# A residual rebuilt on GpSimd from two kept parts, in place of a DRAM copy, in a fused attention and gated-MLP kernel

## Chip, cores and metric

One core of one Trainium2 chip. The metric is the device time of one execution in microseconds (us). The kernel before took 342.78 us, the median of 3 runs (342.32 to 345.28).

## What is computed

Four batches; each has 12 heads of causal attention (448 positions, head size 64), whose output x (768 features of 448 positions) goes through a gated MLP with a residual. `f` below stands for the tanh form of GELU.

```
attn = softmax(mask(q @ k.T / 8)) @ v            # per batch and head
x    = attn as [448, 768]
h    = f(x @ w_in);  u, v = h[:, :512], h[:, 512:]
vn   = (v - mean(v)) / sqrt(var(v) + 1e-6) * g_ln
vs   = w_sg @ vn + b_sg[:, None]
out  = x + (u * vs) @ w_out
```

## The kernel before

The 48 heads go in 24 pairs (0 to 23, six a batch); a pair gives 128 of the 768 feature rows of x. For a pair: one load of q and k (L428); scores on TensorE (PE, L435) in two halves; masked maxima on VectorE (DVE, L450); exponentials on ScalarE (ACT, L458), ten a pair; the inverse sums go through DRAM (rd, L477) and come back spread over the partitions (rb, L480). The probabilities must then be transposed. Pairs 0 to 7 do it on PE (L502) with copies by ACT and DVE. Pairs 8 to 23 use two block transposes on DVE (L490) into one shared buffer (P_92 in the orders below), and four DMAs from it into a slot of B (L494, two slots). PE multiplies B by the values (L528, the "o" matmuls), and DVE scales the result by rb into a tile xt (L555). So from pair 8 on a pair's transposes wait for the four DMAs of the pair before to land, and its DMAs wait for the o matmuls of the pair two before, which held the slot of B.

`keep_x` then keeps a pair's x in two float32r parts, a high part (a rounded copy, by GpSimd, POOL, at L562 in batch 0 and by ACT at L564 later) and a low part (POOL, L565 for 448 columns, L567 for 64 more), in one of six slots. Both parts feed the MLP's matmuls as split products. Beside that, a DMA writes x to a DRAM tile xd (L560).

The MLP of a batch is made of matmul groups (all L584): v groups (`win,x`, 512 wide), u groups (`x,win`, 448), s groups (`wsg,vn`) and o groups (`g,wout`). For the output of each 128 feature rows (`mc`, six a batch) an o group runs on PE, and DVE adds the residual to it (L704). Two mc share one tile `res`: it is read back from xd by a DMA (L692, 448 KB; two slots, in the last batch the slots of qk), added to, and written out (L712 in pairs of mc, in the last batch L708 one by one, its last mc in two halves of 224 columns). Gating uses POOL at L678 and L681.

Nothing is scheduled while it runs. The operations are recorded with their dependences, and a table of numbers, ORDER, gives the order in which they are issued; each engine works its own part of that order strictly one after the other, and so does the DMA queue of SyncE (SP), which issues every load and store. An issue that waits holds up all issues behind it.

Of the kernel before, what the change touches and what calls it, by code (L numbers as in the profile page):

```python
# [8 lines left out]
F32 = mybir.dt.float32  # L9
# [4 lines left out]
ALU = mybir.AluOpType  # L14
# [214 lines left out]
def attention_gated_mlp(ctx: ExitStack, tc: tile.TileContext, qk, vP, w_in, g_ln, w_sgT, b_sg, w_out, out):  # L229
# [47 lines left out]
    rT = [const.tile([8, 128], F32, name=f"rT{i}") for i in range(NS)]  # L277
    pad = const.tile([128, 8], F32, name="pad")
    rd = [dram.tile([128, 128], F32, name=f"rd{i}") for i in range(NS)]
    xd = dram.tile([B, DM, S], F32, name="xd")  # L280

    od = Order(slots)

# [484 lines left out]
```

## Time and profile before

The profile is of one execution of 343.92 us; its span, first to last instruction, is 342.1 us.

| | before |
|---|---|
| median of 3 runs | 342.78 us |
| profiled execution, its span | 343.92 us, 342.1 us |
| PE busy | 328.2 us (96%) |
| DVE, ACT, POOL busy | 256.8, 198.1, 148.5 us |
| DMA queue of SP | 69.06 MB, 68.6% of the 16 engines' span |

Read it in this order: how much PE idles, where, and what ended the idling; then which work stands right ahead of those places in the chain of waits; then what the touched instructions take.

### The profile page before, as it was taken

What the parts mean: (1) busy time and instruction counts of PE and PEld (TensorE: products, weight loads), DVE (VectorE), ACT (ScalarE), POOL (GpSimd) and SP (SyncE); (2) the same over time, 40 slices, a digit from 0 to 9 for tenths busy, and PEclk for the clock granted to TensorE, in tenths of its full rate; (3) what the DMA queues carried; (4) which work ended last, traced back from release to release, by engine and by line L of the source; (5) the groups of instructions that cost most, each with busy time, mean ns of one, the idle gap of its engine ahead of it and who ended that gap; (6) DMA issues with size and microseconds to landing.
All of it is one profiled execution on the core that took longest, in us unless ns stands there. A gap on an engine that the chain in (4) does not pass through costs nothing.

```text
span 342.1 us, 7655 instructions
## 1 busy us (share of the span) xinstructions
PE 328.2 (96%) x2614; PEld 266.9 (78%) x2615; DVE 256.8 (75%) x762; ACT 198.1 (58%) x658; POOL 148.5 (43%) x201
## 2 busy tenths in 40 slices
PE   3998989999999999999999999999998999999995
PEld 2666567777987887878888978878887987799995
DVE  4899887899999899979879776989577431477513
ACT  2999897896657756566644853753562601243410
POOL 4467586678779700302342901202226623142550
PEclk9999999999999999999999999999999999999999
DMA  7979878787688987788698789747676656005304
GB/s 231 347 241 294 273 243 272 209 306 218 170 224 236 283 236 225 223 229 222 164 290 234 225 225 266 205 119 160 187 199 199 192 129 194 0 2 188 107 2 161
DMA packets 37975, 69.55 MB, mean 203 GB/s; under 512 B 3888, under 2 KB 18992, under 8 KB 37936
## 3 DMA queue, kind: packets, MB, share of 16 engines
q1 hardware_dynamic: 37936, 69.06, 68.6%
q8 instruction: 21, 0.34, 0.4%
q14 instruction: 18, 0.15, 0.1%
HBM read 39.68 MB, written 12.58 MB: 153 GB/s over the span
## 4 chain that ended last, share of the span: by engine, by line
PE 79%; ACT 6%; DMA 6%; DVE 4%; issue 1%; SPq 1%; POOL 1%; DVEq 0%; POOLq 0%; ACTq 0%
PE m L584 58%; PE o L528 10%; PE s L435 9%; ACT P L458 4%; DMA vn<-in_w_in_dram 2%; DMA qk<-in_qk_dram 2%; DMA B<-P 2%; PE ty L502 1%; PE tx L502 1%; ACT B L509 1%; ACT vn L370 1%; PE s L472 1%; DVE P L490 1%; SPq L494 1%; DVE s L450 1%
## 5 line engine op out<-in xcount | busy, mean ns | idle before, releaser
L458 ACT ACTIVATE P<-s,ngm 64x64 f32<-64x64 f32 (+3 forms) x240 | 100.4, 429 | 33.2 <-DVE ngm L450 18.3
L450 DVE CUSTOM_DVE_ANT_0 s<-s,mask 128x192 f32<-128x192 f32 (+3 forms) x192 | 77.3, 438 | 8.3 <-PE s L435 7.2
L584 PE MATMUL m<-win,x 128*128 128x512 f32 (+1 forms) x264 | 65.4, 397 | 0.0
L584 PE MATMUL m<-g,wout 128*128 128x448 f32 x288 | 62.0, 369 | 0.0
L584 PE MATMUL m<-x,win 128*128 128x448 f32 x288 | 61.6, 367 | 0.0
L584 PEld LDWEIGHTS m<-x,win 128*128 128x128 f32 x288 | 53.6, 188 | 4.9
L584 PEld LDWEIGHTS m<-g,wout 128*128 128x128 f32 x288 | 53.3, 188 | 5.2
L584 PEld LDWEIGHTS m<-win,x 128*128 128x128 f32 (+1 forms) x264 | 47.1, 183 | 11.3
L435 PE MATMUL s<-qk 64*64 64x64 f32 (+5 forms) x768 | 47.3, 376 | 6.1 <-DMA qk<-in_qk_dram 5.5
L435 PEld LDWEIGHTS s<-qk 64*64 64x64 f32 x768 | 30.4, 140 | 24.4 <-issue 10.4
L458 ACT ACTIVATION_READ_ACCUMULATOR P<-s,ngm 128x1 f32 (+1 forms) x240 | 48.6, 202 | 0.0
L528 PE MATMUL o<-B,vraw 128*64 128x64 f32 (+4 forms) x672 | 45.9, 291 | 1.3 <-issue 1.0
L528 PEld LDWEIGHTS o<-B,vraw 128*64 128x64 f32 x672 | 33.5, 137 | 15.1 <-issue 6.3
L490 DVE STREAM_TRANSPOSE P<-P 128x1024 f32<-128x1024 f32 x32 | 38.5, 1226 | 5.5 <-DMA vraw<-in_vP_dram 2.9
L584 PE MATMUL m<-wsg,vn 128*128 128x448 f32 x176 | 39.0, 368 | 0.3 <-DVE vn L641 0.3
L628 POOL TENSOR_TENSOR mv<-mv,mhalf 128x1 f32<-128x1 f32 (+1 forms) x16 | 10.4, 648 | 58.7 <-DVE mv L626 52.2
L584 PEld LDWEIGHTS m<-wsg,vn 128*128 128x128 f32 x176 | 32.7, 188 | 3.5 <-issue 0.6
L565 POOL TENSOR_TENSOR x<-xt,x 128x448 fp32r<-128x448 f32 x24 | 27.8, 1166 | 17.3 <-ACT x L564 17.0
L595 ACT ACTIVATE tmp<-tmp 128x448 f32<-128x448 f32 (+2 forms) x32 | 19.2, 603 | 16.2 <-DVE tmp L593 15.9
L678 POOL TENSOR_TENSOR tmp<-tmp,g 128x448 f32<-128x448 f32 x16 | 18.2, 1144 | 23.9 <-DVE tmp L674 16.3
L593 DVE SCALAR_TENSOR_TENSOR tmp<-tmp,m 128x448 f32<-128x448 f32 (+1 forms) x28 | 17.6, 632 | 12.3 <-ACT tmp L592 12.2
L450 DVE DVE_READ_ACCUMULATOR2_ANT ngm<- 128x1 f32 (+1 forms) x192 | 26.2, 136 | 0.0
(77 smaller groups left out, 363.0 us busy)
## 6 DMA issues: line engine op xcount, KB each, us to landing
B<-P SPq DMA_DIRECT2D x64, 256.0 KB
qk<-in_qk_dram SPq DMA_DIRECT2D x24, 448.0 KB
vn<-in_w_in_dram SPq DMA_DIRECT2D x12, 512.0 KB
vraw<-in_vP_dram SPq DMA_DIRECT2D x24, 256.0 KB
rb<-rd SPq DMA_DIRECT2D x24, 256.0 KB
xd<-xt SPq DMA_DIRECT2D x24, 224.0 KB
res<-xd SPq DMA_DIRECT2D x9, 448.0 KB
out_dram<-res SPq DMA_DIRECT2D x9, 448.0 KB
```

Source lines behind the costliest of these rows:

```text
L435: nc.tensor.matmul(out=s[z][bk].t[64 * h:64 * h + 64, col:col + n], lhsT=qk_.t[r, 0, q0:q0 + 64], rhs=qk_.t[r, 1, k0:k0 + n], start=True, ...
L450: nc.vector.tensor_tensor_reduce(out=o, in0=i, in1=mk, scale=-0.125, scalar=3e38, op0=ALU.add, op1=ALU.min, accum_out=ngm[ib[z]][c][0:m])
L458: act(n, lambda c=c, m=m, k0=k0, n=n, bk=bk, col=col, off=off, kc=kc, i=i, z=z: nc.scalar.activation(out=P[i][0:m, off:off + n], in_=s[z][ ...
L490: dve(PW, lambda z=z: nc.vector.transpose(A[ia][:, :, :, z, :].rearrange("p g t k -> p t g k"), P[ib[z]]), Pk[z] + [kp], Ak, 1.105)
L502: nc.tensor.transpose(out, P[ib[z]][:, col:col + 128], ident)
L528: nc.tensor.matmul(out=dst(o.t[r]), lhsT=vr.t[:, c, r], rhs=src(z), start=first and n == 0, stop=last and n == len(lst) - 1)
L565: pool_tt(S, lambda: nc.gpsimd.tensor_tensor(out=y.t[:, S + 64:], in0=x.t, in1=f(y.t)[:, 0:S], op=ALU.subtract), [x, y], [(y, 1)])
L584: nc.tensor.matmul(out=ps.t[0:l().shape[1], 0:n], lhsT=l(), rhs=rr(), start=(k == 0), stop=(k == len(mms) - 1))
L593: dve(n, lambda: nc.vector.scalar_tensor_tensor(out=z(), in0=z(), scalar=1.0 / GC, in1=h(), op0=ALU.add, op1=ALU.mult), [ps], [t])
L595: act(n, lambda: nc.scalar.activation(out=z(), in_=z(), func=AF.Tanh, scale=GS * GC), [], [t], True)
L628: od.add("pool", 0.46, lambda mv=mv, m=m: nc.gpsimd.tensor_tensor(out=mv.t[0:m, 1:2], in0=mv.t[0:m, 1:2], in1=mhalf[0:m], op=ALU.pow), ["s ...
L678: pool_tt(S, lambda z=z, u=u: nc.gpsimd.tensor_tensor(out=z(), in0=z(), in1=u.t, op=ALU.mult), [u], [t])
```

## The change

xd goes. `keep_x` no longer writes x to DRAM (24 DMAs of 224 KB), and the residual is no longer read back (12 DMAs of 448 KB). Instead POOL adds the high and the low part of a pair's x into its half of `res` (L691 of the changed kernel, 24 additions of 128x448), and DVE's L704 waits for that half. `res` has three slots in all batches, the last one included. The rb tile is 448 columns instead of 512. A slot of x is now free once the matmuls and the addition have read it.

```diff
-    xd = dram.tile([B, DM, S], F32, name="xd")
...
-        rb, sb = buf(some[SLOTS["rb"]], "rb", [128, 512]), s[1][1]
+        rb, sb = buf(some[SLOTS["rb"]], "rb", [128, S]), s[1][1]
...
-        dma(lambda: nc.sync.dma_start(out=xd[b, hp * 128:(hp + 1) * 128, :], in_=x.t), [x], [("xd", b, hp)], 229e3)
...
-                rr = buf(*((two, "res") if b < B - 1 else (some[SLOTS["qk"]], "qk")), [128, 2, S])
-                dma(lambda rr=rr, d2=d2: nc.sync.dma_start(out=rr.t, in_=xd[b, d2, :].rearrange("(a p) s -> p a s", a=2)),
-                    [("xd", b, mc), ("xd", b, mc + 1)], [rr], 459e3)
+                rr = buf(three, "res", [128, 2, S])
+                for k in range(2):
+                    x = xhl[b, mc + k]
+                    pool_tt(S, lambda rr=rr, x=x, k=k: nc.gpsimd.tensor_tensor(
+                        out=rr.t[:, k, :], in0=f(x.t)[:, 0:S], in1=f(x.t)[:, S + 64:], op=ALU.add), [x, (x, 1)], [(rr, k)],
+                            ring=[rr])
...
-                    [ps, rr], [(rr, 2 * k + z)])
+                    [ps, (rr, z)], [(rr, 2 + 2 * k + z)])
...
-    4, 1, 2, 84, 85, 0, 89, 87, 90, 88, 86, 93, 91, 12, 13, 96, 95, 98, 97, 94, 100, 102, 14, 92, 101, 99, 15, 16, 17,
+    0, 2, 84, 1, 4, 85, 87, 86, 89, 88, 90, 91, 93, 92, 12, 14, 94, 13, 15, 127, 128, 132, 130, 129, 16, 17, 95, 96,
```

The table ORDER is new from its first to its last number (1927 before, 1915 now), so every engine has another order. Three places matter below.

**SP, the moves of the last two pairs into B.** `B<-P_92` is one of a pair's four DMAs into its slot of B, `x2` and `x4` so many behind one another; vraw is a load of values, rd and rb the inverse sums. Before, the stretch with the moves of pairs 22 and 23:

```order
L560 DMA xd<-xt 128x448
L494 DMA B<-P_92 128x1x512 x2
L560 DMA xd<-xt 128x448
L522 DMA vraw<-in_vP_dram 128x512 x2
L692 DMA res<-xd 128x2x448
L494 DMA B<-P_92 128x1x512 x2
L477 DMA rd_128<-rT_124 4x16x128 x2
L480 DMA rb<-rd_128 128x1x512
L494 DMA B<-P_92 128x1x512 x4
L560 DMA xd<-xt 128x448
```

and now, pairs 20 to 23:

```order
L492 DMA B<-P_92 128x1x512 x4
L426 DMA qk<-in_qk_dram 128x896
L492 DMA B<-P_92 128x1x512 x4
L475 DMA rd_126<-rT_122 4x16x128 x2
L475 DMA rd_128<-rT_124 4x16x128 x2
L478 DMA rb<-rd_128 128x1x448
L478 DMA rb<-rd_126 128x1x448
L492 DMA B<-P_92 128x1x512 x4
L520 DMA vraw<-in_vP_dram 128x512 x2
L712 DMA out_dram<-res 128x2x448
L492 DMA B<-P_92 128x1x512 x4
```

Before, pair 22's four moves stood in two pieces with a write to xd, two value loads and a read of `res` between; now each of the last four pairs has its four moves in one piece. Of the 16 pairs five had their moves in pieces before, three have now.

**PE, where pairs 12, 13 and 14 are multiplied.** `o_2284` before and `o_2258` now are pair 13's o matmuls; `o_2270` is pair 14's (`o_2465` before, which follows only 29 rows below the end of this piece). Before:

```order
L584 MATMUL m_2256<-x_1426,win_87 128x448 x3
L584 MATMUL m_2260<-x_1426,win_87 128x448 x3
L584 MATMUL m_2233<-x_1975,win_87 128x448 x3
L584 MATMUL m_2256<-x_1428,win_87 128x448 x3
L528 MATMUL o_2284<-B_2047,vraw_2034 64x256 x2
L528 MATMUL o_2284<-B_2047,vraw_2034 64x128 x2
L528 MATMUL o_2284<-B_2047,vraw_2034 64x64 x2
L528 MATMUL o_2284<-B_2047,vraw_2034 64x256 x2
L528 MATMUL o_2284<-B_2047,vraw_2034 64x64 x2
L528 MATMUL o_2284<-B_2047,vraw_2034 64x128 x2
L528 MATMUL o_2284<-B_2047,vraw_2034 64x64 x4
L435 MATMUL s_2305<-qk_2092 64x448
```

and now:

```order
L581 MATMUL m_2245<-x_1453,win_87 128x448 x3
L581 MATMUL m_2245<-x_1456,win_87 128x448 x3
L581 MATMUL m_2245<-x_1845,win_87 128x448 x3
L581 MATMUL m_2245<-x_1909,win_87 128x448 x3
L526 MATMUL o_2258<-B_2101,vraw_2015 64x256 x2
L526 MATMUL o_2258<-B_2101,vraw_2015 64x128 x2
L526 MATMUL o_2258<-B_2101,vraw_2015 64x64 x2
L526 MATMUL o_2270<-B_2227,vraw_2268 64x256 x2
L526 MATMUL o_2270<-B_2227,vraw_2268 64x128 x2
L526 MATMUL o_2270<-B_2227,vraw_2268 64x64 x2
L526 MATMUL o_2258<-B_2101,vraw_2015 64x256 x2
L526 MATMUL o_2258<-B_2101,vraw_2015 64x64 x2
```

Pair 14's o matmuls have moved up, in between those of pair 13. Between the last o matmul of pair 12 and the first of pair 14 there stand now one pair's scores, 9 matmuls 512 wide, 24 matmuls 448 wide (eight rows of three), one small `s<-ident,rs` and the first six o instructions of pair 13. Pair 11 too is multiplied earlier after its scores: between them stand now the scores of pairs 12, 13 and half of 14, 48 matmuls 448 wide and pair 10's o matmuls.

**POOL, the end of the last batch.** `tmp` and `g` rows are the gating, `res` rows the new additions. Before, the last eight rows of work:

```order
L678 TENSOR_TENSOR tmp_3880<-tmp_3880,g_3825 128x448
L681 TENSOR_TENSOR g_3909<-tmp_3880,g_3907 128x448
L678 TENSOR_TENSOR tmp_3902<-tmp_3902,g_3876 128x448
L681 TENSOR_TENSOR g_3958<-tmp_3902,g_3956 128x448
L678 TENSOR_TENSOR tmp_3933<-tmp_3933,g_3900 128x448
L681 TENSOR_TENSOR g_3976<-tmp_3933,g_3974 128x448
L678 TENSOR_TENSOR tmp_3937<-tmp_3937,g_3905 128x448
L681 TENSOR_TENSOR g_3981<-tmp_3937,g_3979 128x448
```

and now, the last eleven:

```order
L675 TENSOR_TENSOR tmp_3881<-tmp_3881,g_3821 128x448
L678 TENSOR_TENSOR g_3892<-tmp_3881,g_3890 128x448
L675 TENSOR_TENSOR tmp_3902<-tmp_3902,g_3856 128x448
L675 TENSOR_TENSOR tmp_3922<-tmp_3922,g_3886 128x448
L678 TENSOR_TENSOR g_3925<-tmp_3902,g_3905 128x448
L675 TENSOR_TENSOR tmp_3934<-tmp_3934,g_3888 128x448
L678 TENSOR_TENSOR g_3937<-tmp_3922,g_3927 128x448
L678 TENSOR_TENSOR g_3941<-tmp_3934,g_3939 128x448
L691 TENSOR_TENSOR res_3678<-x_3206 128x448
L691 TENSOR_TENSOR res_3997<-x_3631 128x448
L691 TENSOR_TENSOR res_3997<-x_3636 128x448
```

Three of the 24 additions stand behind all gating. On SP the last seven stores were three of 448 columns, the two halves of 224, and two more of 448; now the five of 448 come first and the two halves last.

## Rows read from the trace of the kernel before

**Rows 1.** The page: engine, busy us (share of span), instructions.

```profile
PE 328.2 (96%) x2614; PEld 266.9 (78%) x2615; DVE 256.8 (75%) x762; ACT 198.1 (58%) x658; POOL 148.5 (43%) x201
```

**Rows 2.** Windows: stretch, length, busy us (instructions) by engine, PEclk, DMA share, GB/s.

```profile
12.00:21.00 9.00, 8.38 (x74) 5.58 (x72) 8.16 (x34) 9.00 (x33) 3.97 (x5) 1.00 0.84 274
21.00:46.00 25.00, 22.23 (x252) 15.33 (x251) 21.98 (x85) 23.88 (x95) 15.97 (x20) 1.00 0.87 277
46.00:100.00 54.00, 54.00 (x402) 42.06 (x401) 49.93 (x154) 42.53 (x135) 40.12 (x55) 1.00 0.76 231
...
250.00:300.00 50.00, 48.70 (x345) 41.25 (x343) 24.04 (x53) 15.87 (x42) 18.04 (x21) 1.00 0.53 147
...
330.00:342.10 12.10, 8.62 (x43) 7.65 (x41) 3.78 (x7) 0.00 (x0) 0.98 (x1) 0.94 0.32 115
```

**Rows 3.** PE's waits: line, waited for, us in total, times, longest.

```profile
PE tx L502 <- ACT P L458: 1.2, 1, 1.2
PE o L528 <- issue: 1.0, 1, 1.0
...
PE o L528 <- DMA B<-P: 0.3, 1, 0.3
```

**Rows 4.** Chain that ended last: start us, us, what.

```profile
34.79 7.49 DMA vn<-in_w_in_dram
...
108.52 2.45 PE s L435 x32
...
200.85 2.44 PE m L584 x12
203.29 3.68 PE o L528 x64
...
214.62 10.46 PE m L584 x45
...
257.53 1.04 issue
...
279.45 5.85 DMA B<-P
...
287.42 51.21 PE m L584 x245
338.66 0.62 DVE qk L704
```

**Rows 5.** Timeline of SP's queue: start us, us, instruction, count.

```profile
122.72 3.20 SPq L494 DMA_DIRECT2D B<-P  x4
...
260.96 1.20 SPq L494 DMA_DIRECT2D B<-P  x2
...
266.25 1.20 SPq L494 DMA_DIRECT2D B<-P  x2
...
276.93 4.11 SPq L494 DMA_DIRECT2D B<-P  x4
...
333.84 5.81 SPq L708 DMA_DIRECT2D out_dram<-qk  x7
```

**Rows 6.** Lines L560, L692: ns min/median/max, first and last start.

```profile
L560 SPq DMA_DIRECT2D xd<-xt x24: 325/613/1614, 32.5 to 311.7; - x24
L692 SPq DMA_DIRECT2D res<-xd x9: 371/434/917, 58.7 to 287.0; - x9
```

**Rows 7.** Groups of POOL: line, shapes, count, busy us, mean ns, idle before.

```profile
L565 POOL TENSOR_TENSOR x<-xt,x 128x448 fp32r<-128x448 f32 x24 | 27.8, 1166 | 17.3 <-ACT x L564 17.0
```

**Rows 8.** Lines L704, L490, L372 on DVE: ns min/median/max, first and last start.

```profile
L704 DVE TENSOR_TENSOR qk<-m,qk x7: 381/624/625, 333.2 to 338.7; 128x448 f32<-128x448 f32 x5, 128x224 f32<-128x224 f32 x2
L490 DVE STREAM_TRANSPOSE P<-P x15: 1190/1223/1246, 179.3 to 273.7; 128x1024 f32<-128x1024 f32 x15
L372 DVE TENSOR_SCALAR g<-g x16: 241/248/735, 49.4 to 104.9; 128x192 int32<-128x192 int32 x16
```

More of the change, by code (lines that the diff above doesn't have):

```diff
@@ L295, in dve, with pool_tt @@
         od.add("dve", 0.068 + n * rate / 1000, fn, r, w, done, port=port, ring=ring)
-    def pool_tt(n, fn, r, w):
-        od.add("pool", 0.15 + n * 0.00224, fn, r, w, port=True)
+    def pool_tt(n, fn, r, w, ring=()):
+        od.add("pool", 0.15 + n * 0.00224, fn, r, w, port=True, ring=ring)
     def consts():
@@ L480, in pair @@
         dma(lambda: nc.sync.dma_start(out=rb.t, in_=bass.AP(
-            tensor=rd[ip].tensor, offset=rd[ip].offset, ap=[[512, 32], [0, 4], [1, 512]])), [("rd", ip)], [rb], 262e3, dur=0.56)
+            tensor=rd[ip].tensor, offset=rd[ip].offset, ap=[[512, 32], [0, 4], [1, S]])), [("rd", ip)], [rb], 229e3, dur=0.56)
         Pk = [[("P", i, c) for c in range(5)] for i in ib]
@@ L709, in mlp @@
                                                                                 in_=rr.t[:, z, lo:hi]),
-                        [(rr, 2 * k + z)], [], 512.0 * (hi - lo))
+                        [(rr, 2 + 2 * k + z)], [], 512.0 * (hi - lo))
             if b < B - 1 and z:
                 dma(lambda rr=rr, d2=d2: nc.sync.dma_start(out=out[b, d2, :].rearrange("(a p) s -> p a s", a=2),
-                                                           in_=rr.t), [(rr, 0), (rr, 1)], [], 459e3)
+                                                           in_=rr.t), [(rr, 2), (rr, 3)], [], 459e3)
     weights_a()
```

183 rows, old and new, of the table ORDER are left out of this document.

## The prediction

> **What bounds the kernel now.** The page's busy times come first: TensorE (PE) is busy 328.2 of the 342.1 us of the span, VectorE (DVE) 256.8, ScalarE (ACT) 198.1, GpSimd (POOL) 148.5 [rows 1]. So 342.1 - 328.2 = 13.9 us is all that PE idles, and a change that leaves PE's matmuls as they are can win no more than that. The windows say where it is. From 12 to 21 us ACT is busy 9.00 of 9.00 us, from 21 to 46 us 23.88 of 25.00, and PE has gaps there: the first exponentials bind. From 46 to 100 us PE is busy 54.00 of 54.00. From 250 to 300 us it lacks 1.3 us, and at the end 12.1 - 8.62 = 3.5 us are the last result's way out [rows 2]. The waits and the chain name the late gaps. PE waits 1.0 us at 257.53 before o matmuls, put down to issue, and 0.3 us for a move into B before 285.4 [rows 3, 4]. I read both as one cause: the chain ahead of the second gap is a move into B, 5.85 us from 279.45 to 285.30 [rows 4], and the first gap too stands before o matmuls, which need such moves. One early wait for ACT, 1.2 us, stands behind a late weight load (7.49 us from 34.79) in the chain [rows 3, 4].
>
> **What goes.** On the transfer queue, 24 issues of about 0.61 us and 9 of 0.43, with 3 more like the latter: 24 x 0.61 + 12 x 0.43 = 20 us of SP's time [rows 6]. PE's late waits name neither xd nor `res` [rows 3], so their going is worth only what they held up. They held up moves into B: pair 22's four issues began at 260.96 and ended at 267.45, two and two, with other issues between; without these two pieces, at 1.20 us for two, they take 2.4 us in place of 6.5 [rows 5]. That delays the next pair too, because pairs share one transposed buffer: a pair's cycle is two transposes of 1.22 us [rows 8], then issues and landing, 276.93 to 285.30 or 8.4 us for the last pair [rows 4, 5], together 10.8 us. With the order of before each late pair loses up to 4 us to foreign issues, and the two gaps of 1.0 and 0.3 us are smaller than that. The new order has each of the last four pairs' moves in one piece. I take both gaps as gone: **-1.3 us**; bounds 0 (another wait takes the place) and -1.3.
>
> **The early part.** The table is new, so the early wait of 1.2 us need not recur, but ACT has the same exponentials before the same matmuls, and it is full there. A gain is bounded by the 1.2 us; a loss by about the same, if a like load comes late once. I take **-0.3 us**.
>
> **The end.** Before, DVE's last addition (0.62 us from 338.66) was a full one of 448 columns [rows 4]; now the two halves come last, and a half takes 0.381 us against 0.624 [rows 8]. The store behind it is half the size too; its issue is one of seven in 5.81 us [rows 5], about 0.8 us, and stays. **-0.3 us**; bounds -0.2 and -0.6.
>
> **What comes: 24 additions on POOL.** The nearest row is the subtraction of the same shape, 1166 ns [rows 7]: 24 x 1.166 = 28 us, POOL 148.5 to 176.5 us, with 165 left. Three stand behind the last gating, 3.5 us; their first taker is an o group's addition on DVE, and PE's queue of 245 matmuls, 51.21 us without a gap [rows 4], is the cover: the adds wait for its last groups, not for POOL. I cost them at nothing. Without it the end would slip by up to 1.2 us. A slot of x now also waits for its addition before ACT's copy of a later pair can go; the order puts these additions ahead of the low part of that later pair, and I cost that at nothing too, under PE's long groups between. The fewer bytes (10.8 of 69.06 MB) and rb's 448 columns shorten no wait that PE shows.
>
> DVE can suffer from POOL. One form of DVE's goes up to 735 ns against a median of 248, and something held that instruction up; but the transposes of pairs 17 to 23 never do, 1190 to 1246 ns [rows 8]. The sum by the rows: 24 additions, at most 0.49 us each on some DVE instruction, 12 us on an engine with 85 us to spare, of which I let 0 reach PE.
> The Trainium skill (SBUF — State Buffer, section "🔬 SBUF: two separate sides") says that DVE and GpSimd share one pair of SBUF ports as an exclusive lock, the loser blocked for the whole instruction. By that rule 24 x 1.17 = 28 us of DVE could be blocked; the first pair of numbers above agrees with it, the transposes show nothing of it.
>
> **What the new order makes tighter.** PE's order brings pair 14's o matmuls to right behind pair 13's. Its slot of B is free when pair 12's o matmuls end. Between stand one pair's scores (2.45 us hold one and a half: 1.63), 9 wide matmuls (10.46/45 = 0.232 each: 2.1), 24 narrow ones (2.44/12 = 0.203 each: 4.9) and half of pair 13's o (3.68/2 for a pair, 0.8 for the six) [rows 4]: 9.4 us. Four moves took 8.4 us at the quiet end and, issued in 3.20 us and landing in 5.85, 9.1 in the busy middle [rows 4, 5]; issued in 4.11 us, 10.0. So slack 1.0 to a stall of 0.6.
> Pair 11's o follow its scores after the scores of two and a half pairs (4.1 us), 48 narrow matmuls (9.7) and pair 10's o (1.8): 15.6 us. Before, its scores ended at 108.52 + 1.63 = 110.2, its moves were issued from 122.72, and 8.4 us later, at 131.1, they had landed [rows 4, 5]: 20.9 us, a stall of 5.3 if that were all work. But it holds waiting for pair 10's moves; the part that can't shrink is 2.45 + 8.4 = 10.8 us and the last exponentials. I take **+0.4 us** for both places, near the lower bound, because the two pairs' scores now lie further apart than they did; bounds 0 and +5.9.
>
> **The sum**, on the profiled execution: 342.1 - 1.3 - 0.3 - 0.3 + 0.4 = 340.6. Around the span lay 343.92 - 342.1 = 1.8 us: 342.4. That execution was 343.92 - 342.78 = 1.1 us above the median of its runs, so I forecast **341.2 us**.
>
> **The rivals.**
> - *All waits for transfers go.* The late gaps, 1.3, the end at its bound, 0.6, and of the 3.4 us that PE lacks from 12 to 46 us [rows 2] two thirds, 2.3: 4.2 us; 342.8 - 4.2 = **338.6 us**. For it: transfers stand right ahead of each of these gaps. Against it: ACT is full early.
> - *Hidden anyway.* The late pairs stay on their 10.8 us cycle, another issue or DVE's transposes come late instead, and the gaps only move: **342.8 us**. For it: the 16 pairs' cycles hang on one another up to the last move at 285 us, and the new order gives its early links less room.
> - *Slower: pairs 11 and 14 come late.* If pair 11 still needs its 20.9 us, PE stands 5.3 us, and 0.6 at pair 14; it decides from 15.6 us on. 341.2 - 0.4 + 5.9 = **346.7 us**. For it: before, no pair's B came sooner than the cycle allows. Against: what pair 11 waited for is itself moved.
> - *Slower: POOL blocks DVE in that cycle.* If each of 16 pairs' transposes loses 0.3 us, 16 x 0.3 = 4.8 on the one chain: 341.2 + 4.8 = **346.0 us**. Against: the transposes' times [rows 8].
> The lock of the Trainium skill (SBUF — State Buffer, the same section) is the rule by which this rival would come about.
>
> **How the numbers follow.** Chances: forecast 0.55, all waits go 0.18, hidden 0.17, pairs 11 and 14 0.06, POOL blocks DVE 0.04. The range runs from the second case to most of the slower ones' way, 338.6 to 344.5, and leaves out about 2 in 10. A measurement of this kernel tells about 1%, 3.4 us, from no change: faster means under 339.4, slower over 346.2. Faster: most of the second case and a little of the first, 0.20; slower: 0.08, the two slow rivals short of their best ends; the same: 0.72.
>
> **What would show it.** Right: no gap of PE before o matmuls after 200 us; the last addition of 0.38 us; POOL's additions at about 1.17 us and POOL near 176 us; PE without a wait between 46 and 250 us. Wrong: a wait of PE for a move into B between 105 and 150 us (pairs 11, 14), transposes over 1.3 us, more than 4 us that PE lacks between 12 and 46 us (3.4 before), or a wait of L704 for POOL at the end.

## The result and the profile after

The changed kernel takes 340.08 us, the median of 8 runs (339.32 to 341.17), against 343.25 us (342.06 to 345.28, 8 runs) of the kernel before beside it: a ratio of 0.9909, 95% interval 0.9881 to 0.9938, or 3.1 us less (2.1 to 4.1). The forecast was 1.6 us less, a median of 341.2, range 338.6 to 344.5. The direction held and the time lies in the range; the gain was twice the forecast, and its parts came out quite different from the sum.

The profiled execution took 341.12 us, 1.0 us above the median; its span is 339.3 us. The page of the changed kernel: span, then busy us, share and instructions of each engine, then the group of the new additions.

```profile
span 339.3 us, 7630 instructions
...
PE 326.6 (96%) x2614; PEld 267.5 (79%) x2615; DVE 258.3 (76%) x762; ACT 197.2 (58%) x658; POOL 174.1 (51%) x225
...
L691 POOL TENSOR_TENSOR res<-x 128x448 f32<-128x448 f32 x24 | 27.6, 1166 | 21.5 <-DMA out_dram<-res 21.3
```

POOL went from 148.5 to 174.1 us [rows 1], and an addition takes 1166 ns, just what the subtraction of its shape took [rows 7]. The last part of its line had not been foreseen: 21.3 us, in two waits of 12.6 and 8.8, in which POOL stood ahead of an addition for a `res` slot whose output store had not landed.

The windows of the changed kernel (stretch, length, busy us and instructions of PE, PEld, DVE, ACT, POOL, granted clock, DMA share, GB/s), to lay beside [rows 2]:

```profile
12.00:21.00 9.00, 8.18 (x76) 5.92 (x77) 8.67 (x37) 9.00 (x34) 3.98 (x5) 1.00 0.77 250
21.00:46.00 25.00, 24.14 (x264) 17.37 (x258) 21.88 (x85) 24.97 (x98) 16.99 (x20) 1.00 0.82 259
46.00:100.00 54.00, 52.41 (x425) 40.54 (x424) 49.63 (x157) 40.96 (x129) 40.56 (x55) 1.00 0.67 199
...
250.00:300.00 50.00, 50.00 (x354) 42.68 (x353) 25.43 (x55) 15.28 (x41) 23.92 (x25) 1.00 0.36 103
...
330.00:339.30 9.30, 5.03 (x25) 4.32 (x23) 3.10 (x6) 0.00 (x0) 0.00 (x0) 0.90 0.35 124
```

Between 250 and 300 us PE has no gap any more (50.00 of 50.00, 48.70 before). From 21 to 46 us ACT is full (24.97 of 25.00, 23.88 before) and PE works 1.9 us more, of which 1.6 us is given back as a gap between 46 and 100. And the end is longer: 9.30 - 5.03 = 4.3 us after PE's last matmul, where it was 3.5. PE's waits in the changed kernel, all of those over 0.1 us:

```profile
PE s L433 <- DMA qk<-in_qk_dram: 5.1, 2, 3.9
PE s L433 <- ACT P L456: 1.2, 1, 1.2
PE tx L500 <- ACT P L456: 0.8, 1, 0.8
PE s L470 <- DVE rs L467: 0.5, 1, 0.5
PE o L526 <- DVE B L505: 0.3, 1, 0.3
PE ty L500 <- ACT P L456: 0.2, 1, 0.2
```

Neither of the late waits of [rows 3] is left, and none for a move into B or for `res` has come.

**A measure used below.** Busy time hides matmuls that run slower than their like, so I also took PE's lag: where a row of PE's timeline starts, less the matmul work that the program puts ahead of it, at the prices of rows (0.203 us for a matmul 448 wide, 0.228 for 512, 1.69 for a pair's scores, 1.84 for a pair's o, 0.11 for a small one). All kernels have the same 315.5 us of such work; the lag at the last matmul plus the end is the rest of the span. "200 to end" is the lag gained between 200 us and PE's last matmul, "end" what follows it to the end of the span.

| kernel (one execution each) | lag at 80 us | at 200 us | 200 to end | end |
|---|---|---|---|---|
| before | 17.8 | 20.1 | 3.0 | 3.5 |
| before, second execution (e8) | 17.1 | 19.3 | 3.8 | 3.5 |
| changed kernel | 16.3 | 18.3 | 1.2 | 4.3 |
| e1, changed code, old order | 17.9 | 22.0 | 3.2 | 5.3 |
| e3, moves of 3 pairs together | 16.7 | 19.1 | 1.4 | 3.5 |
| e12, moves of 5 pairs together | 17.8 | 20.8 | 1.8 | 3.5 |
| e4, no additions | 14.7 | 16.7 | 1.0 | 4.2 |
| e5, halves earlier | 14.5 | 16.9 | 1.2 | 4.1 |
| e7, additions twice | 15.4 | 17.7 | 2.0 | 4.3 |
| e9, one pair's moves split | 15.0 | 17.0 | 1.7 | 4.3 |
| e10, old start, changed code | 15.7 | 18.1 | 1.2 | 4.3 |

Between 80 and 200 us the kernels hardly differ, e1 apart (2.0 to 3.0; e1 4.1). The gain lies in the start, some 1.5 to 2 us, and after 200 us, some 2 us; the end gives 0.7 back. Note the scatter in the first column: five executions with the same order and transfers at the start (changed kernel, e4, e5, e7, e9) lie between 14.5 and 16.3.

### The profile page after: what moved, and what is told of

Read it like the earlier page. It is cut to its first block, busy times and chain, and to the rows that moved or that the text cites. A ratio compares the mean times of both kernels' runs of the same rounds, so it can differ in the third digit from the quotient of the medians.

```text
span 339.3 us, 7630 instructions
## 1 busy us (share of the span) xinstructions
PE 326.6 (96%) x2614; PEld 267.5 (79%) x2615; DVE 258.3 (76%) x762; ACT 197.2 (58%) x658; POOL 174.1 (51%) x225
## 3 DMA queue, kind: packets, MB, share of 16 engines
q1 hardware_dynamic: 31216, 57.26, 58.1%
## 4 chain that ended last, share of the span: by engine, by line
PE 83%; ACT 6%; DVE 4%; DMA 4%; issue 1%; SPq 1%; DVEq 0%; ACTq 0%
PE m L581 63%; PE o L526 10%; PE s L433 8%; ACT P L456 5%; DMA rd<-rT 2%; DVE s L448 1%; DMA g<-in_w_out_dram 1%; DMA qk<-in_qk_dram 1%; ACT B L507 1%; ACT vn L368 1%; PE s L470 1%; DVE vn L372 1%; PE tx L500 1%; PE ty L500 1%; DVE vn L370 0%
## 5 line engine op out<-in xcount | busy, mean ns | idle before, releaser
L581 PE MATMUL m<-g,wout 128*128 128x448 f32 x288 | 61.3, 368 | 0.0
L433 PE MATMUL s<-qk 64*64 64x64 f32 (+5 forms) x768 | 46.6, 375 | 6.4 <-DMA qk<-in_qk_dram 5.1
L456 ACT ACTIVATION_READ_ACCUMULATOR P<-s,ngm 128x1 f32 (+1 forms) x240 | 49.9, 208 | 0.0
L526 PEld LDWEIGHTS o<-B,vraw 128*64 128x64 f32 x672 | 33.0, 137 | 13.5 <-issue 5.5
L691 POOL TENSOR_TENSOR res<-x 128x448 f32<-128x448 f32 x24 | 27.6, 1166 | 21.5 <-DMA out_dram<-res 21.3
L581 PE MATMUL m<-wsg,vn 128*128 128x448 f32 x176 | 38.1, 367 | 0.0
L704 DVE TENSOR_TENSOR res<-m,res 128x448 f32<-128x448 f32 (+1 forms) x25 | 14.7, 600 | 19.0 <-PE m L581 19.0
L675 POOL TENSOR_TENSOR tmp<-tmp,g 128x448 f32<-128x448 f32 x16 | 18.3, 1148 | 17.5 <-DVE tmp L671 17.4
```

Source lines behind the costliest of these rows:

```text
L433: nc.tensor.matmul(out=s[z][bk].t[64 * h:64 * h + 64, col:col + n], lhsT=qk_.t[r, 0, q0:q0 + 64], rhs=qk_.t[r, 1, k0:k0 + n], start=True, ...
L456: act(n, lambda c=c, m=m, k0=k0, n=n, bk=bk, col=col, off=off, kc=kc, i=i, z=z: nc.scalar.activation(out=P[i][0:m, off:off + n], in_=s[z][ ...
L526: nc.tensor.matmul(out=dst(o.t[r]), lhsT=vr.t[:, c, r], rhs=src(z), start=first and n == 0, stop=last and n == len(lst) - 1)
L581: nc.tensor.matmul(out=ps.t[0:l().shape[1], 0:n], lhsT=l(), rhs=rr(), start=(k == 0), stop=(k == len(mms) - 1))
L675: pool_tt(S, lambda z=z, u=u: nc.gpsimd.tensor_tensor(out=z(), in0=z(), in1=u.t, op=ALU.mult), [u], [t])
L691: pool_tt(S, lambda rr=rr, x=x, k=k: nc.gpsimd.tensor_tensor(out=rr.t[:, k, :], in0=f(x.t)[:, 0:S], in1=f(x.t)[:, S + 64:], op=ALU.add), [ ...
```

## The experiments

**Is it the code or the order?** Two kernels take the halves of the change apart.

e1 has the changed code in the order of before: the table is that of before with the 36 transfers taken out and each pair of additions put in near the read it replaces (for the last batch, where the slots of `res` allow it, at the end).

> The changed kernel's code (no DRAM copy of x, additions on GpSimd, three residual slots) in the order of the kernel before: the 36 transfers are gone from their places, the 24 additions stand near where the reads stood, all else keeps its place. Theory A (the new order brings the gain, the removed transfers only made room for it): 342.5 to 343.5 us, and the wait of 1.0 us before pair 21's o matmuls and ScalarE's early wait for a weight load are still there. Theory B (the removed transfers and their bytes bring it): 340 to 341 us, both waits gone.

Measured: 346.75 us, ratio 1.0107 (1.0079 to 1.0135), slower than before by 3.7 us. Two of PE's rows of e1's timeline (start us, us, instruction, in brackets the idle time before it and what ended it):

```profile
77.20 3.94 PE L525 MATMUL o<-B,vraw 128*64 128x448 f32 x40 [1.07 <-ACT P L455]
...
260.80 2.44 PE L525 MATMUL o<-B,vraw 128*64 128x256 f32 x44 [1.11 <-issue]
```

The last row of POOL in e1's timeline:

```profile
333.05 6.71 POOL L690 TENSOR_TENSOR res<-x 128x448 f32<-128x448 f32 x6
```

The late gap of 1.0 us at pair 21 [rows 3, 4] is there again, 1.11 us, though no write to xd and no read of `res` stands on SP's queue any more. So it was not their issues that held pair 21 up. What did is on SP's queue of the kernel before, with pair 21's moves:

```profile
246.09 0.56 SPq L494 DMA_DIRECT2D B<-P  x1
246.69 0.59 SPq L428 DMA_DIRECT2D qk<-in_qk_dram  x1
247.34 1.69 SPq L494 DMA_DIRECT2D B<-P  x2
251.79 0.61 SPq L477 DMA_DIRECT2D rd<-rT  x2
252.45 0.93 SPq L494 DMA_DIRECT2D B<-P  x1
```

The fourth move stands behind an issue of rd, which waits 2.7 us for DVE. By the semaphore updates in the traces this move has landed at 258.48 us, and PE goes on at 258.57; in e1 it has landed at 260.71 (rd waits 4.7 us there), and PE goes on at 260.80.

A new wait for ACT has come at 77 us, and six additions stand behind the last gating, so the end takes 5.3 us. The end belongs to where I put the additions, and the wait at 77 us most likely too: e10 below has the same start up to 68 us, where e1 alone has two additions (2.74 us of POOL), and it has no such wait. What else e1 loses between 80 and 200 us was not followed up. What e1 shows without it: the code alone, in the old order, removes no late gap.

e2 is the reverse: the code of before, three `res` slots, in the new order.

> The kernel before (x written to DRAM and read back) in the order of the changed kernel, three residual slots: each write stands behind the low part of its x, each read some 60 operations ahead of where the addition stood. Theory A: 340 to 341 us, as the changed kernel. Theory B: 342.5 us or more, with waits of TensorE before o matmuls, since the 36 transfers stand between the moves into B again.

Measured: 374.6 us, ratio 1.0917 (1.0882 to 1.0952). Far beyond both expectations. DVE's first wait of e2 (waited for, us in total, times, longest):

```profile
DVE xt L554 <- DMA xd<-xt: 33.6, 6, 9.2
```

A write to xd holds its xt slot (two of them) until it has landed, and it stands on SP's queue behind issues that themselves wait for DVE; so DVE's next xt waits, 1.5 us in all before, 33.6 us here, and ACT, POOL and PE behind it. The new order is only possible without the writes, at least where I put them. Neither half is worth anything alone, which neither of my theories had.

**What made the late gaps?** e3 changes only where the moves into B stand, in the kernel before. On SP:

```diff
 L494 DMA B<-P_92 128x1x512 x4
 L480 DMA rb<-rd_126 128x1x512
-L494 DMA B<-P_92 128x1x512
+L494 DMA B<-P_92 128x1x512 x4
 L480 DMA rb<-rd_127 128x1x512
...
-L494 DMA B<-P_92 128x1x512
+L494 DMA B<-P_92 128x1x512 x4
 L428 DMA qk<-in_qk_dram 128x896
-L494 DMA B<-P_92 128x1x512 x2
 L477 DMA rd_127<-rT_123 4x16x128 x2
-L494 DMA B<-P_92 128x1x512
 L560 DMA xd<-xt 128x448
...
-L494 DMA B<-P_92 128x1x512 x2
+L494 DMA B<-P_92 128x1x512 x4
```

> The kernel before, with one edit of its order: the four moves into B of pairs 20, 21 and 22 stand directly behind one another, what stood between them comes after. My theory (the two late gaps come from moves in pieces): the gaps of 1.0 us at 257.5 and 0.3 us at 285.4 go, 341.9 us for a median of 343.2 before. Rival (another chain is as late): the gaps stay or move, 343.2 us.

Measured: 342.34 us, ratio 0.9992 (0.9968 to 1.0016): 0.3 us less, -1.1 to +0.5. Its window from 250 to 300 us:

```profile
250.00:300.00 50.00, 50.00 (x353) 42.51 (x353) 25.43 (x56) 16.75 (x42) 19.85 (x23) 1.00 0.50 144
```

The gaps are gone, and in the table e3 loses 1.4 us after 200 us where before loses 3.0. The transfers of x are all still there. But the times show less than the 1.3 us expected. Two more kernels followed that up. e8 is the kernel before once more.

> The kernel before, unchanged, for a second profile of it: how far its early part, its two late gaps and its end differ from one execution to the next. If the late gaps belong to the kernel: about 1.0 us at 257 us and 0.3 at 285 again. If they belong to that one execution: other or none.

Measured: 343.91 us, one run. PE's rows of its timeline with a late wait:

```profile
204.99 1.99 PE L528 MATMUL o<-B,vraw 128*64 128x256 f32 x32 [0.44 <-DMA B<-P]
258.40 2.44 PE L528 MATMUL o<-B,vraw 128*64 128x256 f32 x44 [0.86 <-DVE g L597]
285.43 1.99 PE L528 MATMUL o<-B,vraw 128*64 128x256 f32 x32 [0.43 <-DMA B<-P]
```

The same two gaps and a third at pair 17. They belong to the kernel. e12 puts the moves of all five pairs together, as e3 did, also those of pairs 8 and 16.

> The kernel before with the moves into B of all five pairs that had them in pieces (8, 16, 20, 21, 22) directly behind one another; all else as before. The one with pairs 20 to 22 alone showed both late gaps gone in its profile, some 1.8 us by TensorE's matmuls, but only 0.3 us in the times (-1.1 to +0.5). If the late gaps cost every execution: 341.0 to 341.6 us, 1.2 to 1.8 us faster than before. If they belong to some executions, or the time is lost again elsewhere: 342.0 to 342.8 us.

Measured: 341.86 us, ratio 0.9952 (0.9928 to 0.9975), 1.6 us less (0.9 to 2.5). Its window from 250 to 300 us:

```profile
250.00:300.00 50.00, 49.92 (x351) 42.09 (x351) 25.81 (x57) 16.94 (x44) 18.55 (x22) 1.00 0.54 154
```

So the pieces make the late gaps, and to have the moves in one piece is worth about 1 us by the times (0.3 us in e3, 1.6 in e12), without the change's code. For the gap at pair 21 e1, e3 and the landing times agree: the foreign issue that counted is that of rd, not a transfer of x. No run moved that issue alone. For the gap at pair 23 no run tells which of the issues between pair 22's moves counted.

e9 tries it from the other side, in the changed kernel, with one pair:

```diff
-L492 DMA B<-P_92 128x1x512 x4
+L492 DMA B<-P_92 128x1x512 x2
 L520 DMA vraw<-in_vP_dram 128x512 x2
 L712 DMA out_dram<-res 128x2x448
-L492 DMA B<-P_92 128x1x512 x4
+L492 DMA B<-P_92 128x1x512 x6
```

> The changed kernel with one edit of its order: two of pair 22's four moves into B stand behind the two value loads and the output store that followed them, as in the kernel before; all else in its place. If moves in pieces cost the late gaps: pair 23's transposes start some 3.5 us later, TensorE waits 2 to 3 us before pair 23's o matmuls at 279 us, 342 to 343 us. If the cycle of the pairs has that much room: no wait and 340.1 us.

Measured: 340.53 us, ratio 0.9936 (0.9911 to 0.9961), which the changed kernel's interval overlaps. SP's row in e9's timeline, with pair 23's moves:

```profile
262.36 11.87 SPq L492 DMA_DIRECT2D B<-P  x6
```

PE's row in e9's timeline, pair 23's o:

```profile
278.32 1.99 PE L526 MATMUL o<-B,vraw 128*64 128x256 f32 x32 [0.23 <-DMA rd<-rT]
```

Pair 23's transposes on DVE, in e9 and in e5, whose lag is about the same and whose moves are whole:

```profile
268.56 2.37 DVE L488 STREAM_TRANSPOSE P<-P 128x1024 f32<-128x1024 f32 x2 [2.12 <-DMA B<-P]
266.29 2.35 DVE L488 STREAM_TRANSPOSE P<-P 128x1024 f32<-128x1024 f32 x2
```

Its moves have been issued at 274.2 us, against 272.0 in e5. So the split did delay the cycle by some 2 us, and PE waits only 0.23 us for it. My expectation of 2 to 3 us was wrong: I had taken the delay of the cycle as PE's wait, where PE had some 2 us of room. One split pair now costs next to nothing; before, five were split, three of them one after another (20, 21 and 22).

**What made the early gain?** e6 is the kernel before with the new order for its first 600 operations.

> The kernel before (x in DRAM, read back) with the changed kernel's order for its first 600 of 1915 operations (some 80 us), each write to DRAM behind the low part of its x, and the order of before for the rest. If the early gain (TensorE some 1.4 us ahead at 80 us) comes from the new order there: 1 to 1.5 us faster than before, 341.3 to 341.9. If it comes from the transfers left out, or is the scatter from one execution to another: no faster than before, 342.5 to 343.5.

Measured: 353.22 us, ratio 1.0299 (1.0263 to 1.0335). PE's longest wait in it is 7.9 us at 91 us, where the two orders join, and belongs to neither. But the start too was no better: from 21 to 46 us PE was busy 22.23 of 25.00, as in the kernel before, and ACT 21.15, less than before (23.88). With the writes to xd in it the new start gains nothing, as in e2.

e10 is the reverse, the order of before for the first 600 operations, but with the changed code.

> The changed kernel's code and order, but with the order of before for its first 600 operations (some 80 us; the writes to DRAM are gone from it). If the early gain comes from the new order of the start: TensorE's matmuls of the first 60 us stand about 2 us later than in the changed kernel, 342 us or more. If it comes from the transfers left out: as the changed kernel, 340.1 us. A wait where the two orders join, at about 85 us, would belong to neither.

Measured: 342.01 us, ratio 0.9971 (0.9951 to 0.9990). The interval lies beyond that of the changed kernel (0.9881 to 0.9938), about 2 us slower. Its window from 21 to 46 us:

```profile
21.00:46.00 25.00, 23.35 (x280) 16.59 (x276) 23.58 (x90) 24.97 (x97) 17.65 (x21) 1.00 0.84 273
```

ACT is full here too, 24.97 us, though the order of the start is the old one. ACT's wait for the weight load, 1.1 us in the kernel before and 0.7 in e3 and e8, went with the transfers, not with the order: e1, without transfers in the old order, has none either. But that wait is not all that the start costs. Two of PE's rows in e10, then the changed kernel's row at that place:

```profile
26.65 1.28 PE L432 MATMUL s<-qk 64*64 64x448 f32 x12 [0.58 <-ACT P L455]
28.70 1.09 PE L499 MATMUL ty<-ident,P 128*128 128x128 f32 x8 [0.78 <-ACT P L455]
...
26.66 0.66 PE L500 MATMUL ty<-ident,P 128*128 128x128 f32 x4 [0.24 <-ACT P L456]
```

The first two waits stand in all six executions with the old start (before, e8, e3, e12, e1, e10: 0.57 to 1.55 us and 0.77 or 0.78 us), with the transfers and without; the six with the new start and the changed code (changed kernel, e4, e5, e7, e9, e11) have one of 0.24 to 0.26 us. At 46 us, the lag is 12.5 to 13.5 us in these six, 14.1 in e10, 15.3 in e1 and 15.4 to 16.2 in the four with the transfers. From there to 60 us the new start gives some 0.8 us of its lead back, the changed kernel's own profile 2.2.

So the new order of the start brings a gain once the transfers are gone, 2 us by the times. By the lag at 80 us e10 (15.7) is inside the changed kernel's scatter (14.5 to 16.3), and it had no wait at the join; but its execution, 340.98 us, was 1.0 us under its median, and the changed kernel's was 1.0 above its own, so the two profiles hide the difference that the times show. How the 2 us divide is open.

**What do the additions cost?** e4 leaves them out.

```diff
-                        out=rr.t[:, k, :], in0=f(x.t)[:, 0:S], in1=f(x.t)[:, S + 64:], op=ALU.add), [x, (x, 1)], [(rr, k)],
...
-                    out=rr.t[:, z, lo:hi], in0=ps.t[:, lo:hi], in1=rr.t[:, z, lo:hi], op=ALU.add),
+                    out=rr.t[:, z, lo:hi], in0=ps.t[:, lo:hi], in1=bB[:, lo:hi], op=ALU.add),
```

> The changed kernel without its 24 additions on GpSimd: the residual is left out, VectorE adds a constant tile of the same size instead. My theory (the additions are hidden): as the changed kernel, 339.8 to 340.4 us. Rival (GpSimd holds VectorE up, or the last additions hold up the end): 337 to 339 us.

Measured: 339.35 us, ratio 0.9898 (0.9867 to 0.9928); the changed kernel's is 0.9909. e7 does each of them twice (a loop of two around the same instruction).

> The changed kernel with each of its 24 additions on GpSimd done twice (28 us more of GpSimd, 202 in all). My theory (hidden): no slower than the changed kernel by more than 0.5 us, save up to 3.5 us if the last three, doubled, come too late for the end. Rival (GpSimd's additions block VectorE's work on the path): 1 to 3 us slower all along, with longer transposes and TensorE waiting before o matmuls.

Measured: 341.6 us, ratio 0.9948 (0.9930 to 0.9966), some 1.3 us more than the changed kernel, the intervals just overlapping. Its additions, in the page's groups:

```profile
L693 POOL TENSOR_TENSOR res<-x 128x448 f32<-128x448 f32 x48 | 55.1, 1155 | 20.8 <-DMA out_dram<-res 18.8
```

The transposes of P in e7 (count, then ns min/median/max of one, and the stretch they lie in):

```profile
L488 DVE STREAM_TRANSPOSE P<-P x32: 1190/1232/1246, 75.9 to 268.7; 128x1024 f32<-128x1024 f32 x32
```

The first 24 additions cost 0.4 us by the ratios, which can't be told from nothing, a second 24 some 1.3. POOL is at 202 us then, and the transposes are as long as ever: at most 1246 ns, as in [rows 8]. POOL's additions do not hold up this chain, even at twice their number.

They do hold other work of DVE. In the changed kernel an addition and an instruction of the normalisation ran together:

```profile
172.90 1.14 POOL L691 TENSOR_TENSOR res<-x 128x448 f32<-128x448 f32 x1
172.96 1.36 DVE L627 TENSOR_SCALAR tmp<-tmp,mv 64x512 f32<-64x512 f32 x1
```

Before and now, all instructions of that line:

```profile
L630 DVE TENSOR_SCALAR tmp<-tmp,mv x16: 525/538/617, 69.8 to 312.3; 128x512 f32<-128x512 f32 x12, 64x512 f32<-64x512 f32 x4
L627 DVE TENSOR_SCALAR tmp<-tmp,mv x16: 507/546/1631, 68.2 to 311.4; 128x512 f32<-128x512 f32 x12, 64x512 f32<-64x512 f32 x4
```

It took 1360 ns in place of some 540 and ended 0.28 us after the addition. Three of DVE's instructions stood like this beside an addition, some 2.5 us in all (the 1631 ns stood beside another of POOL's, L633); in e7 they lost some 4.6 us. Since e4, which has none of it, is only 0.4 us faster by the ratios, no cost of the first 2.5 us shows in the times; whether e7's 1.3 us come from its longer ones no run shows.

**The end.** e5 finishes the group with the two halves two groups earlier, as before.

> The changed kernel with one edit at the end of its order: the o group whose result is cut in two halves is finished two groups before the last, as in the kernel before; the last addition and the last store are full ones. If the two halves at the very end cost time (the changed kernel takes 4.3 us from TensorE's last matmul to the end of the span, the kernel before 3.5): 3.5 us again and 0.7 us faster than the changed kernel, 339.0 to 339.7. If the end is as long for any last store: 4.3 us and no change.

Measured: 340.09 us, ratio 0.9915 (0.9885 to 0.9946), no change. The window of e5's end (columns as in the windows of the changed kernel):

```profile
330.00:337.80 7.80, 3.63 (x18) 3.01 (x17) 1.86 (x5) 0.00 (x0) 0.00 (x0) 0.92 0.41 148
```

With a full store last the end is 7.80 - 3.63 = 4.2 us all the same. In the changed kernel and in e5 the last store lands about as long after PE's last matmul as before (some 2.65 us); the 0.7 us lie behind it, among SyncE's closing instructions. e11 adds 36 small issues to SP, so that it has as many as before (271, against 235 in the changed kernel):

```diff
+                    if b == B - 2:
+                        for k in range(12):
+                            nc.sync.dma_start(out=scr[mc // 2 * 12 + k], in_=gcol)
```

> The changed kernel with 36 more issues on SyncE, 2 KB each, behind the output stores of batch 2 at some 290 to 320 us, where that queue is idle: as many issues as the kernel before has. The end from TensorE's last matmul takes 4.1 to 4.3 us in all kernels of the changed code and 3.5 us in those of the code before, and the difference lies in SyncE's own last instructions. If the number of SyncE's instructions sets it: 3.5 us again, 339.4 us. If not: 4.2 us and 340.1 us.

Measured: 350.71 us, ratio 1.0225 (1.0193 to 1.0257). The window of e11's end:

```profile
340.00:348.70 8.70, 5.11 (x26) 4.39 (x24) 3.09 (x6) 0.00 (x0) 0.00 (x0) 0.93 0.37 132
```

Here the end is 8.70 - 5.11 = 3.6 us. SyncE's closing drains, before, changed kernel, e11 and e1:

```profile
L764 SPq DRAIN  x3: 7/7/7, 341.4 to 341.7; - x3
L764 SPq DRAIN  x3: 7/7/130, 338.5 to 338.9; - x3
L769 SPq DRAIN  x3: 7/7/7, 347.9 to 348.3; - x3
L763 SPq DRAIN  x3: 7/7/7, 345.2 to 345.5; - x3
```

By the semaphore updates the last store has landed 0.15 us ahead of the first drain in the kernel before, 0.7 in the changed kernel, 0.14 in e11 and 0.26 in e1. e1 has 235 issues like the changed kernel, and no long closing: its 5.3 us go to the stores that come late. So the number of issues alone doesn't set it; what does stays open. But e11 lost 10 us elsewhere. PE's row with its longest late wait, in e11's timeline:

```profile
312.41 2.61 PE L582 MATMUL m<-wsg,vn 128*128 128x448 f32 x6 [4.80 <-DVE tmp L595]
```

POOL's row just before it, an addition that waited:

```profile
309.55 1.13 POOL L692 TENSOR_TENSOR res<-x 128x448 f32<-128x448 f32 x1 [12.31 <-DMA out_dram<-res]
```

The small transfers delayed an output store; an addition on POOL waited 12.3 us for that store's `res` slot; behind it on POOL stood L626, which batch 3's normalisation needs, and PE stood 4.8 us, then 2.3 more ahead of 324 us for the same normalisation. Between them PE also ran slower (columns as above):

```profile
310.00:316.00 6.00, 3.59 (x10) 3.20 (x11) 3.98 (x8) 1.26 (x2) 4.12 (x5) 0.50 0.06 2
```

From 310 to 316 us the granted clock was 0.50, the lower of its two levels, after PE had stood since 307.6; the matmuls of 448 take some 0.4 us there in place of 0.2. The wait for a slot of `res` is what the change has brought, and here it decides. In the changed kernel the same kind of wait, 21.3 us of POOL, has nothing urgent behind it: without the additions the kernel is only 0.4 us faster (e4).

## Why the prediction was right, and where not

- **What bounds it** held: PE's matmuls, ACT at the start, the moves into B late, the way out at the end.
- **Late gaps, -1.3 us.** They went; the lag puts the gain at about 2 us, the times of e3 and e12 at 0.3 and 1.6. The place and the pieces were right (e3, e12), the cause only in part: I had credited the transfers of x as well, as what stood between the moves. e1 has those gone and keeps the gap at pair 21; e3 and e12 keep the transfers and lose the gaps. The order of the moves did it. I had also taken both gaps for pair 22's split: its moves begin at 260.96 us, after the first gap at 257.53, which was pair 21's.
- **The start, -0.3 us.** This is the term that was most mis-sized. I had bounded it by the one early wait of 1.2 us and taken a quarter; it was 1.5 to 2 us by the lag, and 2 us by the times between e10 and the changed kernel. The load that came late shared its queue with the writes, and its wait on ACT went with them, in the old order too (e1, e10). The order brought more than that: PE's two waits for ACT at 27 and 29 us, 1.3 us together or more in each old start, which I had not counted, are 0.24 us in the new one. That ACT is full early did not forbid a gain.
- **The end, -0.3 us.** Wrong in sign, +0.7 to 0.8. I had also misread the order: the two halves are of one group, so both additions follow PE's last matmul, 0.39 and 0.38 us in place of 0.62. e5 shows that this matters nothing; what came was a longer closing on SyncE, which nothing in the rows before announced.
- **The additions, 0.** Right within what the times tell (e4), and the transposes stayed at 1194 to 1247 ns in the changed kernel. The wait for the output store, which an addition on POOL brings with it, was missed. I had asked what the additions delay, not what they wait for. That some of DVE's instructions would be held, without a cost that shows, was foreseen.
- **Pairs 11 and 14, +0.4 us.** Neither was late: PE waits for no move into B. The bound of 5.3 us for pair 11 had counted the wait for pair 10 as work, as the prediction says: pair 10's moves are now issued from 108.04 us (111.80 before), and pair 11's from 118.89 (122.72 before).
- **The lock.** The rival in which POOL blocks DVE's transposes fell: 24 additions and 48 left them at 1.25 us at most. The rule of the Trainium skill (SBUF — State Buffer, "🔬 SBUF: two separate sides") is of an operation with two SBUF inputs or in a two-port mode on DVE, and the traces agree in so far as an addition holds some of DVE's instructions until it is done (1360 ns in place of 540), while the transposes, which have one input, show nothing of it. In which mode the held ones ran no run shows.
- **Small slips.** The sum gives 341.3 us where 341.2 was written, and the bytes that go are 11.0 MB, not 10.8 (11.8 with those of rb: 69.06 to 57.26). Nothing rests on either.

The sum now: 1.5 to 2 at the start, 2 late, 0.7 given back, against 3.1 measured. That the time came out in the range, though two terms were too small and one had the wrong sign, is in part luck. Open: how the 2 us of the start divide, why e3 gained less in its times than e12, and what lengthens the closing.

## What to carry to other kernels

When a change comes with a new order, take the two apart before crediting either: here each alone, as I built it, was slower than before, by 4 and by 32 us, and only together were they faster by 3. A transfer that is hidden still holds a slot and a place in an in-order queue, and what it holds up shows only as a wait of somebody else; and work moved to a quiet engine brings its own waits there, so ask what stands behind it on that engine when its buffer is late.

## What the runs showed of the hardware

From the landing of the last store to the end the program took 1.5 to 1.6 us in six kernels with 36 fewer transfers on SyncE's queue (the changed kernel, e4, e5, e7, e9, e10), and 0.9 us in those with as many as before, e11 with its 36 small ones included; e1, with 36 fewer, took 1.0. The cause was not found.

And 36 transfers of 2 KB, in rows of 16 bytes, in a stretch where the queue was all but idle, were enough to cost 10 us: one larger store landed late among them, PE stood 4.8 and 2.3 us, and some of its matmuls ran at a granted clock of 0.50.

An addition on POOL held an instruction of DVE until 0.28 us after its own end, three times in the changed kernel, and never a stream transpose (1194 to 1247 ns beside 24 additions, 1190 to 1246 beside 48).
